# A fused attention and mixture-of-experts kernel: a new order of issue in the first head pair and at the seam between its two halves

## The chip, the cores and the metric

The kernel runs on one core of a Trainium2 chip. A core has TensorE (PE: matmuls; its weight loads, PEld, are listed apart), VectorE (DVE), ScalarE (ACT) and GpSimd (POOL). SyncE (SP) only issues DMAs here. Each engine works through its own instruction stream in order, and engines wait for each other by semaphores. The metric is the time of one run in device microseconds (us); the median of three runs of the kernel before is 529.62 us (529.43 to 530.06).

## The reference, cut to what matters

```
scores = cap * tanh(q @ k.T / sqrt(64) / cap)            # 4 batches, 12 heads, 448 rows, cap 30
attn   = softmax(scores);  x = (attn @ v) as 1792 rows of 768
logits = x @ w_gate;  e_idx = argmax(logits)             # 8 experts, one per row
gate_w = softmax(logits)[e_idx];  eom = sigmoid(x @ w_output_gate)
for e: rows = (e_idx == e)
       out[rows] = gate_w * eom[:, e] * (relu(x[rows] @ w1[e]) @ w2[e])   # 768 -> 1024 -> 768
```

All of it is float32.

## The kernel before, in words

**Attention.** Two heads are worked together as a pair; there are 24 pairs u = 0 to 23, six for each batch. `t_k` and `t_q` turn K and Q of a pair with PE (tiles tk, tq) and split them into a high and a low part (KH, KL, QH, QL). `qk(u, s)` for s = 0 to 3 makes the scores of three double chunks and one single chunk in one of two PSUM buffers `s`, and ACT takes their tanh into `th`, which frees that buffer. The exponentials that turn `th` into `pt` are queued in `pend_exp`, and `flush_exp` issues them, two after every second tanh. `pv(u, c)` multiplies with V into `u`; `u_evac` copies that to `ut` (on ACT for pairs 18 to 21 and 23, on DVE for the others). `presum` adds up the exponentials for the softmax sums, on POOL up to pair 21 and on DVE for pairs 22 and 23, and `sums` reduces them on PE (tile sm).

The transposes of pair u + 2 are issued behind pair u, those of pairs 1 to 3 by hand: in before, those of pair 1 stand behind `qk(0, 2)`.

**Routing.** When a batch is done, `end_of_batch` divides by the sums (rec), makes the gate logits (tg, pg, gm, lg), picks experts, gives every row a place, and writes the row to the DRAM table xs (`row_tr` turns it on PE as trow, `row_out` multiplies on DVE as xr and issues the store) and its place to the tables tab. For batches 0 to 2 these steps are hung into the attention loop by numbers: step x of batch b is run in `slot` at 4·6·(b+1) + 4 + x, four slots to a pair, halves being places in between. For batch 3 the list STEPS gives the order: one word is run behind each chunk of the first expert matmuls.

**Experts.** The rows are grouped in blocks of 128 of one expert. The first five blocks hold rows of batches 0 to 2 only; `early` plans them during pair 21 in six steps (the numbers NXP), so that they can start as soon as attention ends. For a block, `fetch_dma` reads its part of the tables (tc), `gather` works out the row numbers and reads the rows from xs by an indirect DMA on POOL (xg), and `tx` turns and splits them (pt_x, then xh by ACT, xl by DVE). Weights come by `load_raw` on SP (raw, 512 KB a chunk for w1) and are split by ACT and DVE into two planes (wr), several chunks ahead of PE. Blocks 0 and 1 run together (`two1`, tiles php and py).

**The seam** is the passage from pair 22 to `two1`. In before, the SP queue holds there: two row stores, the table reads of blocks 0 and 1, the first weight chunk, V of pair 23, three row stores, five weight chunks. PE holds: the last scores, `pv` of pair 22, `pv` of pair 23, and only then `tx(0)`. Framework pools hand out the buffers; the order on each engine is that of the program text, with no scheduler in between. SP's DMAs use eight semaphores in turn, so a ninth waits for the first.

Of the kernel before, what the change touches and what calls it, by code (L numbers as in the profile page):

```python
# [21 lines left out]
def tile_kernel(ctx: ExitStack, tc, q, k, v, cap, w_gate, w_ogate, w1, w2, out):  # L22
    nc = tc.nc
    B, H, S, D = q.shape
# [5 lines left out]
    NU = B * NP  # L30
    REG = 15 * 128
    NTAB = 128 + E * REG
    NSLOT = 18
    NE = 5
# [16 lines left out]
    AH = 6  # L51
    PZ = 4
    RWP = (9, 10, 12, 13, 14)
    NXP = (7, 7, 7, 7, 7, 7)
    F1 = 5
    F2 = 4
    PRE = 3
    STEPS = 'g s S G x0 X1 l2 c rp3 n4 n5 q e n n n n n n zh'
    WARM = (32, 8, 12, 0)
    RB = 7  # L60
    SP0 = 3
# [2 lines left out]
    UACT = 18  # L64
# [33 lines left out]
    NK = 3  # L98
    SK = NK * 128
# [5 lines left out]
        eng.memset(t[0:64, NK, 1], 0.0)  # L105
        eng.memset(t[64:128, NK, 0], 0.0)

    def load_kv(dst, src, u):
        b, p = divmod(u, NP)
        nc.sync.dma_start(out=dst[:, 0:NK], in_=src[b, 2 * p:2 * p + 2, 0:SK].rearrange("j (p c) d -> p c j d", c=NK))  # L110
        for j in range(2):
            nc.sync.dma_start(out=dst[64 * j:64 * j + 64, NK, j], in_=src[b, 2 * p + j, SK:S])

    def load(u):
        if u >= NU:
            return
        b, p = divmod(u, NP)
        a = ldp.tile([CP, NCH, 2, D], F32, tag="lq", name="lq")
        load_kv(kks[u % 2], k, u)
        nc.sync.dma_start(out=a, in_=q[b, 2 * p:2 * p + 2].rearrange("j (p c) d -> p c j d", c=NCH))  # L120
        ldq[u] = a

# [8 lines left out]
    for t in kks:  # L131
        zero(t, nc.vector)
    load(0)
    nc.sync.dma_start(out=capc, in_=cap.to_broadcast([128, 1]))
    wt = const.tile([128, 1], F32, name="wt")
    nc.scalar.activation(out=wt, in_=wz[:, 0:1], func=ACTF.Exp)

# [140 lines left out]

    pend_exp = []

    def flush_exp():
        while pend_exp:
            dst, th = pend_exp.pop(0)
            nc.scalar.activation(out=dst, in_=th, func=ACTF.Exp, scale=capc)  # L284

    def qk(u, s):
        KH, KL, QH, QL = pl[u]
        if s == 0:
            pt[u] = ptp.tile([128, 2 * NK + 1, S], F32, tag="pt", name="pt")
        n = 2 if s < NK else 1  # L290
        sl = slice(s * 128, (s + 1) * 128)
        ps = ps_s.tile([128, 2, 512], F32, tag="s", name="s")
        if s < NK:
            for i, (x, y) in enumerate(((KH, QH), (KL, QH), (KH, QL))):
                for j in range(2):
                    h = slice(64 * j, 64 * j + 64)
                    nc.tensor.matmul(ps[:, j, 0:S], lhsT=x[h, sl], rhs=y[h], start=(i == 0), stop=(i == 2))  # L297
        else:
            for i, (x, y) in enumerate(((KH, QH), (KL, QH), (KH, QL))):
                nc.tensor.matmul(ps[:, 0, 0:S], lhsT=x[:, sl], rhs=y, start=(i == 0), stop=(i == 2))  # L300
        th = thp.tile([128, 2, S], F32, tag="th", name="th")
        nc.scalar.activation(out=th[:, 0:n], in_=ps[:, 0:n, 0:S], func=ACTF.Tanh, scale=icap)  # L302
        pend_exp.append((pt[u][:, 2 * s:2 * s + n], th[:, 0:n]))
        if s % 2:
            flush_exp()

    def pv(u, c):
        P = pt[u]
# [25 lines left out]

    def u_evac(u):
        t = utp.tile([128, S], F32, tag="ut", name="ut")
        if UACT <= u < NU - 2 or u == NU - 1:
            nc.scalar.activation(out=t, in_=ups.pop(u), func=ACTF.Copy)  # L338
        else:
            nc.vector.tensor_copy(out=t, in_=ups.pop(u))  # L340
        ut[u] = t

    def sums(u):

        b, p = divmod(u, NP)
        if p % 2 == 0:
            return
        r = p // 2
        if r == 0:
            smt[b] = ps_m.tile([128, S], F32, tag="sm", name="sm")  # L350
        for g in range(4):
            nc.tensor.matmul(smt[b][32 * g:32 * g + 32], lhsT=ohc[:, r, :], rhs=s1[u - 1 + g // 2][:, g % 2],
                             start=(r == 0), stop=(r == NP // 2 - 1))
# [10 lines left out]
    def end_of_batch(b):  # L364
# [133 lines left out]
        if b < B - 2:  # L498
            at = {1: [t[2], t[3]], 2: [sums_out], 5: [t[1]], 6: [rws[0]], 9: [gts[0]], 10: [rws[1]], 13: [gts[1]], 14: [rws[2]],
                  15: [logits], 16: [choose], 18: [rws[3]], 21: [rank_mm, place], 22: [rws[4]], 23: [place2], 24: [enter]}  # L500
            at.setdefault(26 if b < B - 3 else 22, []).append(rws[5])
        elif b == B - 2:
            g = early()
            nx = P(next, g, None)
            lds = [P(load_raw, 0, w, c) for w in range(2) for c in range((KD, KF)[w])]
            fd = [P(fetch_dma, i) for i in range(NE)]
            at = {-1: [sums_out], 1: [t[2], t[3]], 2: [t[1], *gts], 3: [logits], 4: [choose],
                  6: [rws[0]], 6.5: [rank_mm, place, place2, enter]}
            for i, x in enumerate(RWP, 1):
                at.setdefault(x, []).append(rws[i])  # L510
            for i, x in enumerate(NXP):
                at.setdefault(x, []).append(nx)
            for x, fs in ((10.5, [fd[0], fd[1], P(set_known, NE), lds[0]]), (15, [P(gather, 0), *lds[1:6], fd[2]]),
                          (16, [P(gather, 1), fd[3], *lds[6:]])):
                at.setdefault(x, []).extend(fs)
        if b < B - 1:
            for x, fs in at.items():
                for f in fs:
# [1 line left out]
            return  # L520
        nx = P(next, late_steps, None)
        do = dict(g=t[2], s=t[0], S=t[1], G=t[3], x=gts[0], X=gts[1], l=logits, c=choose, r=rank_mm, p=place, q=place2,
                  e=enter, n=nx, z=L(P(set_known, NSLOT), P(fetch_dma, NE)), h=lambda: next(rests(), None))
        do.update({str(p): rws[p] for p in range(NP)})
        return [L(*[do[x] for x in w]) for w in STEPS.split()]

# [148 lines left out]
    def rests():  # L675

        full, h, hx, wo = rt["rest"]
        sh = [1, 2, NO, E]
        oh, o2 = M("roh", sh), M("ro2", sh)
        two = lambda x: x.unsqueeze(2).to_broadcast(sh)  # L680
        own = lambda i: metah[:, i, NW:].rearrange("a (z n) -> a z n", z=2)
        tt(wo, wo, over(full, NW), ALU.mult)
        tt(oh, two(hx), irow[:, 0:NO].unsqueeze(1).unsqueeze(3).to_broadcast(sh), ALU.is_equal)
        red(metah[:, 2, 0:NW], wo, ALU.max)
        tt(oh, oh, two(h), ALU.mult)
        tt(o2, oh, full.unsqueeze(1).unsqueeze(1).to_broadcast(sh), ALU.mult)
        red(own(1), oh, ALU.max)
        red(own(2), o2, ALU.max)
        tt(o2, oh, e8.unsqueeze(1).unsqueeze(1).to_broadcast(sh), ALU.mult)
        red(own(0), o2, ALU.max)  # L690
        yield
# [41 lines left out]
            nc.sync.dma_start(out=t4[:, c], in_=tabs[c][bass.ds(off, 128)])  # L733

    def gather(i):
        t4 = tcs.pop(i)
        t = xgp.tile([128, 2], F32, tag="tb", name="tb", bufs=6)
        nc.gpsimd.tensor_tensor(out=t4[:, 0:2], in0=t4[:, 0:2], in1=t4[:, 2:4], op=ALU.add)
        nc.gpsimd.tensor_tensor(out=t, in0=t4[:, 0], in1=t4[:, 1], op=ALU.add)
        ti = xgp.tile([128, 1], U32, tag="ti", name="ti", bufs=6)  # L740
        nc.gpsimd.tensor_scalar(out=ti, in0=t[:, 0:1], scalar1=float(NT), scalar2=None, op0=ALU.add)
        tb[i] = (t, ti)
        n = (B - 1) * S if i < NE else NT + 8
        g = xgp.tile([128, DM], F32, tag="xg", name="xg")
        if i in (1, 3, 4):

            nc.gpsimd.memset(g, 0.0)
        nc.gpsimd.indirect_dma_start(
            out=g, out_offset=None, in_=xs[0:n], in_offset=bass.IndirectOffsetOnAxis(ap=ti, axis=0),
            bounds_check=n - 1, oob_is_err=i not in (1, 3, 4))  # L750
        xg[i] = g
# [13 lines left out]
    def tx(i):  # L765
        if i < NSLOT:
            xg[i] = tr_split(xg[i], KD, "x", 2, xgp)
# [61 lines left out]
    def step():  # L829
        if bg:  # L830
            bg.pop(0)()
# [24 lines left out]
    def slot(u, s):  # L856
        for f in slots.pop(4 * u + s, ()):
            f()

    for u in range(NU):  # L860
        if u > 2:
            load(u + 3)
        qk(u, 0)
        qk(u, 1)
        if u > 0:
            presum(u - 1, 1)
        slot(u, 0)
        if u > 0:
            pv(u - 1, 0)
            pv(u - 1, 1)  # L870
            pv(u - 1, 2)
        if u > 1 and u - 2 != EARLY:
            sums(u - 2)
        slot(u, 1)
        if u in (1, 2):

            prep(u + 1)
            load(u + 3)
        qk(u, 2)
        if u == 0:  # L880
            prep(1)
            load(3)
        slot(u, 2)
        qk(u, 3)
        if u > 0:
            pv(u - 1, 3)
            u_evac(u - 1)
        slot(u, 2.5)
        if u > 1:
            prep(u + 2)  # L890
        if u - 1 == EARLY:
            sums(u - 1)
        load_v(u + 2)
        presum(u, 0)
        slot(u, 3)
# [248 lines left out]
    bg.extend(end_of_batch(B - 1))  # L1144
    pv(u, NK)
    u_evac(u)
    tx(0)
    step()
    sums(u)
    step()  # L1150
    gather(2)

# [92 lines left out]
```

## Time and profile before

| | us |
|---|---|
| median of 3 runs | 529.62 |
| the profiled execution, its own time | 527.99 |
| its span, first to last instruction | 526.3 |
| PE busy | 508.1 (97%) |
| ACT busy | 381.6 (73%) |
| DVE busy | 345.5 (66%) |
| POOL busy | 298.7 (57%) |

The span runs from the first to the last instruction; about 1.7 us of the execution's own time lie around it. Busy time is an average over stages with different limits, so it says little about what an edit in one stage is worth: that is read from the rows of the stage. A clock of 1.00 in the profile is TensorE's full speed, 0.51 about half of it. In a timeline row, the text in brackets is the idle time of the engine just before it and what ended that. "x2" merges instructions that follow each other.

### The profile page before, as it was taken

The numbers are of one execution on the slowest core, as the hardware profiler recorded it, in microseconds if no ns is written. First come the engines' busy times: TensorE is split into PE (matmuls) and PEld (weight loads), VectorE is DVE, ScalarE is ACT, GpSimd is POOL, SyncE is SP. The second block draws the span as 40 slices with busy tenths as digits, with TensorE's granted clock in tenths as the row PEclk, the third lists the DMA queues.
The fourth block names the chain that finished last, engine by engine and source line by source line (L and its number), as shares of the span: only waits on it lengthen the run. The fifth ranks groups of instructions, "written<-read, shape, count | busy, mean of one in ns | idle before, by whom it ended". The sixth has DMA issues, their size and how long they took to land. (4 is left out here: it accounts for less than half of the span.)

```text
span 526.3 us, 10342 instructions
## 1 busy us (share of the span) xinstructions
PE 508.1 (97%) x3197; PEld 361.5 (69%) x3197; DVE 345.5 (66%) x576; ACT 381.6 (73%) x498; POOL 298.7 (57%) x341
## 2 busy tenths in 40 slices
PE   7999999999999989699999999999999999999995
PEld 6555465555655544377999898887878968666692
DVE  3363354965496877599998996975758686545460
ACT  5989897888787978535678886886766787555561
POOL 8988967778987696435254975314737015182001
PEclk9999999999999999899999999999999999999999
DMA  6644434445445316887159636329659959994001
GB/s 148 142 108 102 105 74 106 103 108 111 102 113 132 73 36 189 289 303 219 49 184 389 243 95 206 128 69 386 242 169 391 375 173 368 359 349 167 1 31 49
DMA packets 106189, 91.94 MB, mean 175 GB/s; under 512 B 80770, under 2 KB 88970, under 8 KB 106128
## 3 DMA queue, kind: packets, MB, share of 16 engines
q1 hardware_dynamic: 97392, 58.48, 38.2%
q0 software_dynamic: 8736, 32.74, 17.2%
q8 instruction: 27, 0.44, 0.3%
q14 instruction: 34, 0.28, 0.2%
HBM read 123.68 MB, written 12.04 MB: 258 GB/s over the span
## 5 line engine op out<-in xcount | busy, mean ns | idle before, releaser
L947 DVE TENSOR_TENSOR wr<-raw,wr 128x768 fp32r<-128x768 f32 (+1 forms) x167 | 172.0, 1067 | 68.3 <-ACT wr L946 59.4
L946 ACT ACTIVATE wr<-raw 128x768 fp32r<-128x768 f32 (+1 forms) x167 | 150.2, 936 | 33.0 <-DMA raw<-in_moe_w_dram 12.1
L302 ACT ACTIVATE th<-s,icap 128x896 f32<-128x896 f32 x96 | 84.3, 915 | 27.4 <-PE s L297 19.0
L284 ACT ACTIVATE pt<-th,capc 128x896 f32<-128x896 f32 x96 | 85.7, 947 | 0.0
L968 PE MATMUL py<-wr,hh 128*128 128x384 f32 x352 | 77.3, 340 | 0.0
L968 PE MATMUL php<-wr,xh 128*128 128x512 f32 x264 | 74.8, 404 | 0.0
L1037 POOL DMA_INDIRECT out_dram<-yo,ti x13 | 18.5, 1426 | 86.6 <-ACT yo L1035 62.2
L968 PEld LDWEIGHTS py<-wr,hh 128*128 128x128 f32 x352 | 61.2, 188 | 4.0 <-issue 3.7
L317 PE MATMUL u<-pt,vv 128*64 128x448 f32 x288 | 59.4, 548 | 0.5 <-ACT ut L338 0.5
L968 PEld LDWEIGHTS php<-wr,xh 128*128 128x128 f32 x264 | 47.6, 189 | 12.9 <-issue 2.1
L329 POOL TENSOR_TENSOR pb<-pa,pt 128x896 f32<-128x896 f32 x22 | 46.5, 2113 | 17.0 <-issue 13.7
L333 POOL TENSOR_TENSOR pb<-pb,pt 64x448 f32<-64x448 f32 x44 | 52.1, 1185 | 4.5 <-DMA tab<-ent,posi 1.2
L328 POOL TENSOR_TENSOR pa<-pt 128x896 f32<-128x896 f32 x22 | 46.3, 2104 | 2.3 <-ACT ex L439 0.8
L968 PE MATMUL py<-wr,hl 128*128 128x384 f32 x176 | 44.8, 335 | 0.0
L968 PE MATMUL php<-wr,xl 128*128 128x512 f32 x132 | 41.4, 395 | 0.0
L317 PEld LDWEIGHTS u<-pt,vv 128*64 128x64 f32 x288 | 18.5, 136 | 30.5 <-issue 23.1
L1084 POOL DMA_DIRECT2D rh<-in_moe_w_dram x42 | 23.5, 561 | 22.7 <-issue 16.3
L297 PE MATMUL s<-QH,KH 64*128 64x448 f32 x144 | 31.7, 432 | 1.7 <-ACT th L302 1.7
L968 PEld LDWEIGHTS py<-wr,hl 128*128 128x128 f32 x176 | 31.8, 188 | 0.0
L340 DVE COPY ut<-u 128x448 f32<-128x448 f32 x19 | 11.8, 623 | 29.9 <-PE u L320 29.1
L968 PEld LDWEIGHTS php<-wr,xl 128*128 128x128 f32 x132 | 24.7, 187 | 6.0
L1138 POOL DMA_INDIRECT out_dram<-yh,toh x6 | 6.0, 1008 | 38.0 <-ACT wr L946 10.0
(243 smaller groups left out, 862.6 us busy)
## 6 DMA issues: line engine op xcount, KB each, us to landing
raw<-in_moe_w_dram SPq DMA_DIRECT2D x78, 512.0 KB
raw<-in_moe_w_dram SPq DMA_DIRECT2D x104, 384.0 KB
rh<-in_moe_w_dram POOLq DMA_DIRECT2D x18, 512.0 KB
rh<-in_moe_w_dram POOLq DMA_DIRECT2D x24, 384.0 KB
lq<-in_q_dram SPq DMA_DIRECT2D x24, 224.0 KB
kk<-in_k_dram SPq DMA_DIRECT2D x24, 192.0 KB
vv<-in_v_dram SPq DMA_DIRECT2D x24, 192.0 KB
xs<-xr SPq DMA_DIRECT2D x18, 224.0 KB
```

The source lines that it names most:

```text
L284: nc.scalar.activation(out=dst, in_=th, func=ACTF.Exp, scale=capc)
L297: nc.tensor.matmul(ps[:, j, 0:S], lhsT=x[h, sl], rhs=y[h], start=(i == 0), stop=(i == 2))
L302: nc.scalar.activation(out=th[:, 0:n], in_=ps[:, 0:n, 0:S], func=ACTF.Tanh, scale=icap)
L317: nc.tensor.matmul(ups[u][64 * j:64 * j + 64], lhsT=V[:, c, j, :], rhs=P[:, 2 * c + j], start=(c == 0), stop=False)
L328: eng.tensor_tensor(out=a, in0=P[:, 0:2], in1=P[:, 2:4], op=ALU.add)
L329: eng.tensor_tensor(out=s1[u], in0=a, in1=P[:, 4:6], op=ALU.add)
L333: eng.tensor_tensor(out=s1[u][h, j], in0=s1[u][h, j], in1=P[h, 2 * NK], op=ALU.add)
L946: nc.scalar.activation(out=t[:, 0, 0:F], in_=raw, func=ACTF.Copy)
L947: nc.vector.tensor_tensor(out=t[:, 1, 0:F], in0=raw, in1=t[:, 0, 0:F].bitcast(F32), op=ALU.subtract)
L968: nc.tensor.matmul(ps[g][:, 0:n], lhsT=st[:, c], rhs=w[:, z, g * n:(g + 1) * n], start=(c == 0 and st is hi and z == 0), stop=(c == (KD, K ...
L1037: nc.gpsimd.indirect_dma_start(out=out, out_offset=bass.IndirectOffsetOnAxis(ap=ti, axis=0), in_=y, in_offset=None, bounds_check=NT - 1, o ...
L1084: nc.gpsimd.dma_start(out=d, in_=src[bass.ds(e, 1)].rearrange("e (k p) f -> p (e k) f", p=128)[:, c], **kw)
```

## The change

In the first pair, the two small DMAs of the first K load and the load of `cap` are issued by ACT and no longer by SP; PE makes the transposes of pair 1 ahead of `qk(0, 2)`; and after the second tanh ACT makes one exponential, not two.

At the seam, two of the planner's six steps come two and three slots later, behind row stores; the table reads of block 1, its gather and weight chunks 1 to 5 come behind the last three row stores; block 0's row numbers are worked out earlier on POOL (`index`), apart from its gather (`take`); `tx(0)` stands ahead of `pv` of pair 23; the `ut` copy of pair 21 goes from ACT to DVE; `sums(23)` becomes a step of STEPS, behind the first chunk of `two1`; and STEPS puts the last two row stores and the late planner's steps elsewhere.

```
-    NXP = (7, 7, 7, 7, 7, 7)
+    NXP = (7, 7, 7, 7, 9, 10)
-    STEPS = 'g s S G x0 X1 l2 c rp3 n4 n5 q e n n n n n n zh'
+    STEPS = 'g U s S G x0 X1 l2 c 3r p4 n5 n q e nn n n nn zh'
-    def load_kv(dst, src, u):
+    def load_kv(dst, src, u, eng=None):
...
         for j in range(2):
-            nc.sync.dma_start(out=dst[64 * j:64 * j + 64, NK, j], in_=src[b, 2 * p + j, SK:S])
+            (eng or nc.sync).dma_start(out=dst[64 * j:64 * j + 64, NK, j], in_=src[b, 2 * p + j, SK:S])
...
-        load_kv(kks[u % 2], k, u)
+        load_kv(kks[u % 2], k, u, nc.scalar if u == 0 else None)
...
-    nc.sync.dma_start(out=capc, in_=cap.to_broadcast([128, 1]))
+    nc.scalar.dma_start(out=capc, in_=cap.to_broadcast([128, 1]))
...
-    def flush_exp():
-        while pend_exp:
+    def flush_exp(keep=0):
+        while len(pend_exp) > keep:
...
         if s % 2:
-            flush_exp()
+            flush_exp(int((u, s) == (0, 1)))
...
-        if UACT <= u < NU - 2 or u == NU - 1:
+        if UACT <= u < NU - 3 or u == NU - 1:
...
-            for x, fs in ((10.5, [fd[0], fd[1], P(set_known, NE), lds[0]]), (15, [P(gather, 0), *lds[1:6], fd[2]]),
-                          (16, [P(gather, 1), fd[3], *lds[6:]])):
+            for x, fs in ((10.5, [fd[0], P(set_known, NE)]), (11, [lds[0], P(index, 0)]), (14, [fd[1]]),
+                          (15, [P(take, 0), fd[2], *lds[1:4]]), (16, [P(gather, 1), *lds[4:6], fd[3], *lds[6:]]),
+                          (18.5, [P(tx, 0)])):
...
     def gather(i):
+        index(i)
+        take(i)
+
+    def index(i):
...
+    def take(i):
+        ti = tb[i][1]
...
-        qk(u, 2)
         if u == 0:
             prep(1)
             load(3)
+        qk(u, 2)
...
     u_evac(u)
-    tx(0)
-    step()
-    sums(u)
     step()
     gather(2)
```

Three places, as the engines' streams show them. First ACT at the start of the program, a piece of the difference (KH and QH are the first pair's split, th the tanhs, pt the exponentials):

```order
+L112 DMA kk_126<-in_k_dram 64x64 x2
+L134 DMA capc<-in_cap_dram 128x1
 L136 ACT_TABLE_LOAD
 L136 ACTIVATE wt<-wz 128x1
...
 L302 ACTIVATE th<-s,icap 128x896 x2
-L284 ACTIVATE pt<-th,capc 128x896 x2
-L302 ACTIVATE th<-s,icap 128x896
-L302 ACTIVATE th<-s,icap 128x448
-L284 ACTIVATE pt<-th,capc 128x896
+L284 ACTIVATE pt<-th,capc 128x896
+L302 ACTIVATE th<-s,icap 128x896
+L302 ACTIVATE th<-s,icap 128x448
+L284 ACTIVATE pt<-th,capc 128x896 x2
```

ACT now issues three DMAs before anything else, and the second exponential stands behind the third and fourth tanh.

Then PE at the seam, a piece of the difference (the first L320 row ends `pv` of pair 22, the two rows on vv_130 are `pv` of pair 23, tg and sm belong to the last batch's gates and sums):

```order
 L320 MATMUL u<-pt,vv_129 128x448
+L768 MATMUL pt_x<-ident,xg 128x128 x6
 L317 MATMUL u<-pt,vv_130 64x448 x6
 L320 MATMUL u<-pt,vv_130 128x448
-L760 MATMUL pt_x<-ident,xg 128x128 x6
 L389 MATMUL tg<-ut,wg 32x448 x4
+L976 MATMUL php<-wr,xh 128x512 x4
+L976 MATMUL php<-wr,xl 128x512 x2
 L352 MATMUL sm<-pb,ohc 32x448 x4
```

The six transposes of block 0 moved ahead of the whole `pv` of pair 23, and the first expert chunk ahead of the last sums.

Last SP at the seam, before, from the last of the eight table reads that stand there (tc) to weight chunk 1 (raw_1):

```order
L733 DMA tc<-tab_111 128x2
L703 TENSOR_LOAD meta
L703 ISA x2
L710 ISA
L710 DMA raw_0_112<-in_moe_w_dram 128x1024
L110 DMA vv_130<-in_v_dram 128x6x64
L112 DMA vv_130<-in_v_dram 64x64 x2
L490 DMA xs<-xr 448x1x128 x3
L710 ISA
L710 DMA raw_1_113<-in_moe_w_dram 128x1024
```

and now, from the last of four table reads on:

```order
L734 DMA tc<-tab_111 128x2
L110 DMA vv_130<-in_v_dram 128x6x64
L112 DMA vv_130<-in_v_dram 64x64 x2
L704 TENSOR_LOAD meta
L704 ISA x2
L711 ISA
L711 DMA raw_0_112<-in_moe_w_dram 128x1024
L490 DMA xs<-xr 448x1x128 x3
L731 TENSOR_LOAD meta
L731 ISA x2
L734 ISA
L734 DMA tc<-tab_108 128x2
```

Four table reads instead of eight stand ahead of the three row stores. Behind them come eight table reads, and only then weight chunk 1, which stood right behind the stores.

## Rows read from the trace of the kernel before

**Rows 1.** Busy time by stretch: us, PE, PEld, DVE, ACT, POOL, PEclk, DMA share, GB/s.

```profile
26.00:178.00 152.00, 151.13 (x974) 85.40 (x970) 92.10 (x171) 128.26 (x158) 124.71 (x81) 1.00 0.46 102
178.00:212.00 34.00, 30.88 (x184) 16.01 (x182) 25.96 (x76) 27.50 (x39) 24.10 (x21) 1.00 0.47 125
211.70:216.20 4.50, 0.14 (x2) 0.12 (x2) 3.35 (x4) 2.21 (x3) 2.95 (x3) 1.00 1.02 356
217.00:220.40 3.40, 3.40 (x17) 0.86 (x18) 1.02 (x2) 1.36 (x4) 1.50 (x4) 0.51 0.38 102
220.40:270.00 49.60, 48.59 (x262) 40.76 (x262) 44.61 (x118) 27.86 (x39) 16.88 (x24) 1.00 0.55 177
270.00:520.00 250.00, 250.00 (x1593) 202.18 (x1591) 170.78 (x188) 174.23 (x233) 104.65 (x138) 1.00 0.63 229
```

**Rows 2.** Who waited for whom, PE, whole run: us in total, times, longest.

```profile
PE pt_x L760 <- DMA xg<-xs,ti: 4.4, 1, 4.4
PE s L297 <- ACT th L302: 1.7, 2, 1.2
PE tk L271 <- DVE xr L487: 1.6, 2, 1.2
```

**Rows 3.** Timeline of PE, first pairs: start us, us, instruction, idle before it.

```profile
6.27 0.61 PE L258 MATMUL tq<-ident,lq 112*128 112x112 f32 x4 [0.29 <-DMA lq<-in_q_dram]
...
13.40 0.47 PE L297 MATMUL s<-QH,KH 64*128 64x448 f32 x2 [1.21 <-ACT th L302]
...
20.65 0.48 PE L297 MATMUL s<-QH,KH 64*128 64x448 f32 x2
```

**Rows 4.** Timeline of ACT, first pairs.

```profile
8.69 1.91 ACT L302 ACTIVATE th<-s,icap 128x896 f32<-128x896 f32 x2 [1.23 <-PE s L297]
10.49 1.97 ACT L284 ACTIVATE pt<-th,capc 128x896 f32<-128x896 f32 x2
...
19.20 1.53 ACT L302 ACTIVATE th<-s,icap 128x896 f32<-128x896 f32 x2 [0.17 <-PE s L297]
```

**Rows 5.** Timeline of PE at the seam.

```profile
208.33 2.48 PE L317 MATMUL u<-pt,vv 128*64 128x448 f32 x12
210.74 1.02 PE L320 MATMUL u<-pt,vv 128*128 128x448 f32 x2
216.12 0.85 PE L760 MATMUL pt_x<-ident,xg 128*128 128x128 f32 x6 [4.36 <-DMA xg<-xs,ti]
216.89 1.72 PE L389 MATMUL tg<-ut,wg 128*32 128x448 f32 x8
```

**Rows 6.** Timeline of SP's DMA issues at the seam.

```profile
194.50 5.16 SPq L733 DMA_DIRECT2D tc<-tab  x8
200.47 0.34 SPq L710 DMA_DIRECT2D raw<-in_moe_w_dram  x1
...
203.06 1.98 SPq L490 DMA_DIRECT2D xs<-xr  x3
205.26 3.31 SPq L710 DMA_DIRECT2D raw<-in_moe_w_dram  x5
```

**Rows 7.** Timeline of POOL at the seam.

```profile
192.94 2.35 POOL L333 TENSOR_TENSOR pb<-pb,pt 64x448 f32<-64x448 f32 x2
...
199.74 4.33 POOL L333 TENSOR_TENSOR pb<-pb,pt 64x448 f32<-64x448 f32 x2
...
209.00 1.14 POOL L748 DMA_INDIRECT xg<-xs,ti  x1 [3.43 <-DMA raw<-in_moe_w_dram]
```

**Rows 8.** Timeline of DVE at the seam.

```profile
204.26 0.69 DVE L836 CAST wr<-raw 128x1024 fp32r<-128x1024 f32 x1 [1.19 <-DMA raw<-in_moe_w_dram]
...
208.98 1.15 DVE L328 TENSOR_TENSOR pa<-pt 128x896 f32<-128x896 f32 x1
...
212.75 2.36 DVE L947 TENSOR_TENSOR wr<-raw,wr 128x1024 fp32r<-128x1024 f32 x2
...
221.77 2.36 DVE L947 TENSOR_TENSOR wr<-raw,wr 128x1024 fp32r<-128x1024 f32 x2 [3.33 <-ACT wr L946]
```

More of the change, by code (lines that the diff above doesn't have):

```diff
@@ L522, in end_of_batch @@
         do = dict(g=t[2], s=t[0], S=t[1], G=t[3], x=gts[0], X=gts[1], l=logits, c=choose, r=rank_mm, p=place, q=place2,
-                  e=enter, n=nx, z=L(P(set_known, NSLOT), P(fetch_dma, NE)), h=lambda: next(rests(), None))
+                  e=enter, n=nx, U=P(sums, NU - 1), z=L(P(set_known, NSLOT), P(fetch_dma, NE)), h=lambda: next(rests(), None))
         do.update({str(p): rws[p] for p in range(NP)})
```

## The prediction

> **What bounds the kernel now.** I read the stage table first [rows 1]: PE is busy 151.13 of 152 us in attention, 250 of 250 us in the experts, 48.59 of 49.60 behind the seam. ACT and DVE have room nearly everywhere; in 220 to 270 DVE is at 44.61 of 49.60, which I keep for later. So PE's own waits are the time that can be won, and the list of waits over the whole run names them [rows 2]: 4.4 us once for the gathered rows of block 0 (xg), 1.7 for tanhs, 1.6 for row products (xr). Then I read the timelines at the two places that the change touches. At the seam `pv` of pair 23 ends at 211.76 (210.74 + 1.02), and PE stands until 216.12 [rows 5]. From 217.0 to 220.4 the granted clock is 0.51, that is 1.2 in place of 2.4 GHz, and 1.00 ahead of that [rows 1]: at half speed 3.40 us do 1.73 us of work, so the wait costs another 1.67 us. In the first pair PE waits 1.21 us for a tanh at 13.40 [rows 3]; ACT runs without a pause from 8.69 to 19.20, but for 0.17 us [rows 4].
>
> The change aims at all of these. What each part is worth follows, in the times of the profiled execution.
>
> **First pair.** The three DMAs that leave SP bring the first Q load forward; PE's `tq` waits 0.29 us for that load [rows 3], so the first tanh comes 0.3 earlier. On ACT the three issues stand ahead of work that is idle until 5.5 us, so I price them at nothing; without that cover they would cost about three issues of 0.34 us [rows 6]. Next, one exponential (half of 1.97 with overlap, 0.93) moves behind the third tanh [rows 4], which is what PE waits for at 13.40: the wait of 1.21 shrinks by 0.93, and with the 0.3 PE is 1.23 us ahead. That holds only while ACT keeps up, and ACT's total work is the same: its chain is ahead only by 0.3 and by the pause of 0.17, 0.47 in all. The next place where PE needs it is 20.65 [rows 3]: the tanh at 19.20 would start at 18.73 and end 0.96 later (half of 1.91), at 19.7, so PE starts there 0.95 earlier. The transposes of pair 1, moved ahead, fill PE's waits and add nothing. Behind 20.65 PE has no wait for ACT left, so the lead stays. Ends: 0.47 (ACT sets all) to 1.23; I take 0.95, worked out for the very row.
>
> **Seam, when the gather starts.** The gather of block 0 is issued at 209.00 after 3.43 us of waiting [rows 7]. The profile puts this down to a weight load, but by the program it waits for the row stores of batch 2, since it reads xs. The last three are issued until 205.04 (203.06 + 1.98) [rows 6], so the stores land 3.96 us after the last issue. In the new order half of the eight table reads (2.58 of 5.16 us) is no longer ahead of them: 202.46. SP also begins earlier, since the two planner steps now stand behind the row products for which it (and PE, 1.2 us) waits [rows 2]; I take 1.2 for that: 201.3, and landed at 205.2, or 206.4 without it. POOL must be free too: its two additions take from 199.74 to 204.07, and the row numbers another 1.5 until 205.57 (209.00 - 3.43). The row numbers now come first, and wait for four table reads that are issued earlier; the additions took 2.35 at the pair before and 4.33 here [rows 7], so POOL is free between 203.6 and 205.6. The gather starts at about 204.8 (bounds 203.6 and 206.4).
>
> **When it lands.** Before, 7.12 us passed from its issue to PE's start, while five weight chunks (2.6 MB), issued from 205.26 on, kept the DMA full at 356 GB/s [rows 1, 6]. Now these are issued behind eight table reads, some 5 us after the stores. Bounds: 7.12, and 2.24 (1.14 of issue, and 0.39 MB at 356 GB/s). The nearest row is the weight chunk issued into a light queue: issued at 200.47, used by DVE at 204.26, 3.8 us [rows 6, 8]; a gather issues 0.8 longer (1.14 against 0.34) and moves a quarter less (0.3 us): 4.3. So `tx(0)` starts at 209.0 or so, 7.1 us earlier than 216.12.
>
> That is not all gain: `pv` of pair 23 (208.33 to 211.76, 3.43 us) used to run ahead of the wait and now runs behind it [rows 5]. Net 3.7 us. The bounds: PE itself can reach `tx(0)` at 206.6 at the earliest (208.33 less 1.2 for xr and 0.5 for a copy that moves from ACT to DVE), 6.1 us net; with 206.4 and 7.12 it is 213.5 and a loss of 0.8. In both cases what PE wins ahead of `tx(0)` only makes its wait there longer, so I don't add it. Behind the waiting PE stand `pv(23)`, the gate products and the first chunk; the sums' products change places with that chunk, at no cost while planes are ready.
>
> **The clock.** PE's wait is then 209.0 - 206.6 = 2.4 us. A wait of 1.2 us (for xr) left the clock at 1.00 in 178 to 212, one of 4.36 brought it to 0.51 [rows 1, 2]. 2.4 lies between, a little nearer to the short one: I take 1.0 of the 1.67 us as won back; ends 0 and 1.67.
>
> **VectorE behind the seam.** DVE's `xl` now waits for `tx(0)` and stands ahead of the sums of pair 23 (208.98 to 212.75, 3.8 us), and these ahead of the splits that feed PE [rows 8]. Before, DVE then stood 3.33 us until 221.77; this hole can take most of it. Upper end: all 3.8 are paid, since DVE is at 90% until 270 [rows 1]. Lower end: a gain of 1.0, all of PE's idle time in that stretch (49.60 - 48.59), as the planner's later steps and the table entry now come behind `two1`. I take a loss of 1.0. The longer STEPS way of the planner costs nothing as long as blocks 5 and up are not due, 40 us later; the weight chunks issued 1 to 2 us later are covered by several chunks of lead, and would otherwise cost PE that much.
>
> **Sum.** -0.95 - 3.7 - 1.0 + 1.0 = -4.65 us. The profiled execution took 527.99 (a span of 526.3 and 1.7 around it), so about 523.3 there. It lies 1.6 under the median of the runs shown; carried over to that, 529.62 - 4.65 gives 525.0.
>
> **Rivals.**
>
> *The gather lands late all the same.* If the weight chunks weren't what held it up, their absence saves little. For: between its issue and `tx(0)` the 0.39 MB needed only 1.1 us at 356 GB/s of the 7.12. Against: the lone chunk's 3.8 us. If the gather only shared the DMA half and half, it loses 1.1 us to the chunks and takes 6.0 now: `tx(0)` at 210.8, 5.3 earlier, net 1.9, a wait of 4.2 us and so no clock won: -0.95 - 1.9 + 1.0 = -1.85, 527.8. (The Trainium skill, "DMA: Bandwidth & Descriptors", section on queues, rings and completion order, says just that: each DMA engine goes round its queue rows packet by packet, so that POOL's ring would not stand behind SP's backlog. By that rule the time is 527.8; no row here separates the two.)
>
> *VectorE takes it back.* All 3.8 are paid and the clock still falls: -0.95 - 3.7 + 3.8 = -0.85, 528.8, which is no change that can be measured. For: 44.61 of 49.60. Against: the hole of 3.33.
>
> *Slower: PE waits with `pv(23)` behind it.* If `tx(0)` comes less than 3.43 us earlier, PE loses by the new order what it had as filler. With the start's 0.95 and DVE's 1.0 the point is a `tx(0)` later than 212.6; at 214.8 (the stores landing no earlier, with part of the weight backlog again in front) it is -0.95 + 2.1 + 1.0 = +2.15, 531.8. For: POOL was busy or waiting without a break from 199.74 on, and its additions may stretch again. Against: SP is rid of 2.58 us for certain.
>
> **Chances.** The forecast 0.60 (its own range 522 to 527), the late gather 0.18 (527 to 528.6), VectorE 0.12 (528 to 530), slower 0.10 (530.5 to 533). The range 521.8 to 529.6 leaves out the slower case and some 5% below. A difference of 0.2% (1.06 us) is about what a measurement of this kernel can tell. Faster by more: 0.58 + 0.16 + 0.04 = 0.78; slower by more: the slower case and 0.01 of VectorE's, 0.11; the same: 0.11.
>
> **What would show it.** In the new profile PE starts the row at 20.65 about 1 us earlier, and the list of waits has no 1.2 for xr at the seam. The three row stores are issued by 201.3 less the start's lead, the gather near 204, `tx(0)` near 208 with a wait of 1.5 to 3.5 in front. A clock of 1.00 through the seam, or a shorter stretch at half speed, shows that term; new PE waits for DVE between 210 and 240 would show VectorE's. The forecast is wrong if the gather still takes over 6 us to land, or if PE's waits return as many small ones in `two1`.

## The result: 0.9% slower, and the profile after

The changed kernel takes 534.64 us (median of 6 runs) against 530.02 for the kernel before in the same session: a ratio of 1.0088, 95% interval 1.007 to 1.0105. The prediction had 525.0 and ended its range at 529.6, so it was wrong in sign. The profiled execution has a span of 532.8 us (526.3 before).

First PE's list of waits, as in [rows 2] (us in total, times, longest). The 4.4 for the gathered rows (xg) has fallen to 1.2. In its place stand waits that were small or absent: 4.3 at once for xr, 2.4 for ble, 1.7 for ut, 1.6 for xl.

```profile
PE tq L258 <- DVE xr L487: 4.5, 2, 4.3
PE ph L976 <- DVE ble L536: 2.4, 1, 2.4
PE tg L389 <- ACT ut L338: 1.7, 1, 1.7
PE pt_x L768 <- DVE xl L770: 1.6, 1, 1.6
PE pt_x L768 <- DMA xg<-xs,ti: 1.2, 1, 1.2
```

Next the stage table, as in [rows 1] (us, PE, PEld, DVE, ACT, POOL, PEclk, DMA share, GB/s). PE's idle time in 178 to 212 grew from 3.1 to 5.3 us, in 220.4 to 270 from 1.0 to 4.1; attention before it and the experts behind it stayed full. The half clock (1.2 in place of 2.4 GHz) left the seam and came back behind the two longest of the new waits: 0.50 in 194.3 to 198.8, 0.58 in 249.8 to 253.7.

```profile
26.00:178.00 152.00, 151.16 (x975) 85.57 (x974) 91.36 (x171) 128.75 (x159) 125.63 (x82) 1.00 0.47 103
178.00:212.00 34.00, 28.72 (x165) 15.78 (x163) 27.49 (x73) 24.85 (x35) 21.14 (x21) 0.90 0.35 83
194.34:198.84 4.50, 4.50 (x20) 3.16 (x20) 3.70 (x6) 2.40 (x3) 4.34 (x3) 0.50 0.25 52
220.40:270.00 49.60, 45.53 (x237) 36.05 (x236) 38.20 (x95) 25.42 (x37) 14.20 (x20) 0.97 0.55 182
249.80:253.70 3.90, 3.90 (x11) 3.06 (x12) 1.50 (x7) 0.00 (x0) 0.67 (x1) 0.58 0.54 183
270.00:520.00 250.00, 250.00 (x1591) 205.23 (x1590) 177.92 (x212) 177.06 (x234) 105.07 (x140) 1.00 0.62 228
```

Then the timeline of PE at the places of [rows 3] and [rows 5] (start us, us, instruction, idle before it). The lead at 20 us is 0.65, and it is still 0.65 at 183 us. `tx(0)` comes at 213.13, 2.99 earlier than before; but `pv` of pair 23 and a wait for ut follow, and the first expert chunk (php) starts at 219.90, only 0.13 ahead of 220.03. From there to block 2's first product (ph) it takes 29.9 us, against 25.7 before; these are the rows of before:

```profile
220.03 1.32 PE L968 MATMUL php<-wr,xh 128*128 128x512 f32 x4
...
245.75 0.39 PE L968 MATMUL ph<-wr,xh 128*128 128x512 f32 x1
```

and these the rows now:

```profile
20.00 0.47 PE L297 MATMUL s<-QH,KH 64*128 64x448 f32 x2 [0.28 <-ACT th L302]
...
194.34 1.01 PE L258 MATMUL tq<-ident,lq 112*128 112x112 f32 x4 [4.29 <-DVE xr L487]
...
213.13 0.88 PE L768 MATMUL pt_x<-ident,xg 128*128 128x128 f32 x6 [1.25 <-DMA xg<-xs,ti]
...
219.01 0.96 PE L389 MATMUL tg<-ut,wg 128*32 128x448 f32 x8 [1.66 <-ACT ut L338]
219.90 1.20 PE L976 MATMUL php<-wr,xh 128*128 128x512 f32 x4
...
249.80 0.48 PE L976 MATMUL ph<-wr,xh 128*128 128x512 f32 x1 [2.43 <-DVE ble L536]
```

What held xr up stands in DVE's timeline. These are planner steps five and six, in the places that the change gave them:

```profile
187.99 2.13 DVE L536 TENSOR_TENSOR boh<-boh,bo 1x40 f32<-1x40 f32 x1
190.15 2.12 DVE L543 SCALAR_TENSOR_TENSOR bo<-irow,bval 1x40 f32<-1x40 f32 x1
192.30 1.17 DVE L536 TENSOR_TENSOR bo<-bo,boh 1x40 f32<-1x40 f32 x1
193.50 0.18 DVE L533 TENSOR_REDUCE meta<-bo 1x5 int32<-1x40 f32 x1
193.62 0.67 DVE L487 TENSOR_TENSOR xr<-trow,rec 112x512 f32<-112x512 f32 x1
...
194.77 2.05 DVE L536 TENSOR_TENSOR meta<-bch,bsm 1x4 int32<-1x4 f32 x1
```

Forty numbers take 2.13 us; the same operation took 0.19 at 185.95. POOL's timeline beside it:

```profile
187.97 2.10 POOL L328 TENSOR_TENSOR pa<-pt 128x896 f32<-128x896 f32 x1
190.15 2.07 POOL L329 TENSOR_TENSOR pb<-pa,pt 128x896 f32<-128x896 f32 x1
192.30 2.33 POOL L333 TENSOR_TENSOR pb<-pb,pt 64x448 f32<-64x448 f32 x2
194.70 2.10 POOL L328 TENSOR_TENSOR pa<-pt 128x896 f32<-128x896 f32 x1
```

Each long DVE instruction ends within 0.05 us of a POOL addition (190.12 and 190.07, 192.27 and 192.22, 196.82 and 196.80; 193.47 is where the first of the two halves ends). The reduction and xr, which reads PSUM, are not slowed. The kernel before shows one such case in the planner, not among its rows above; here is DVE's row, and below it POOL's, which starts 0.08 us earlier:

```profile
188.67 2.04 DVE L535 TENSOR_TENSOR meta<-bch,bsm 1x4 int32<-1x4 f32 x1
```

```profile
188.59 2.10 POOL L328 TENSOR_TENSOR pa<-pt 128x896 f32<-128x896 f32 x1
```

The Trainium skill states this, "SBUF — State Buffer", section "Who interferes with whom": a DVE instruction with two SBUF inputs contends with a GpSimd instruction that reads SBUF, and the one that comes second blocks until the other is done. The trace agrees, with 2.04 to 2.13 us against 0.19.

### The profile page after: what moved, and what is told of

Its sections match the earlier page's. It is cut to its first block, busy times and chain, and to the rows that moved or that the text cites. A ratio compares the mean times of both kernels' runs of the same rounds, so it can differ in the third digit from the quotient of the medians.

```text
span 532.8 us, 10342 instructions
## 1 busy us (share of the span) xinstructions
PE 510.3 (96%) x3197; PEld 363.2 (68%) x3197; DVE 349.6 (66%) x577; ACT 382.6 (72%) x497; POOL 294.5 (55%) x341
## 5 line engine op out<-in xcount | busy, mean ns | idle before, releaser
L1045 POOL DMA_INDIRECT out_dram<-yo,ti x13 | 19.8, 1527 | 88.8 <-ACT yo L1043 63.8
L333 POOL TENSOR_TENSOR pb<-pb,pt 64x448 f32<-64x448 f32 x44 | 50.1, 1139 | 4.1 <-DMA tab<-ent,posi 0.8
L474 POOL DMA_INDIRECT tab<-ent,posi x16 | 15.6, 975 | 24.1 <-DVE ent L472 14.5
```

The lines of the kernel that those rows point to most:

```text
L333: eng.tensor_tensor(out=s1[u][h, j], in0=s1[u][h, j], in1=P[h, 2 * NK], op=ALU.add)
L1045: nc.gpsimd.indirect_dma_start(out=out, out_offset=bass.IndirectOffsetOnAxis(ap=ti, axis=0), in_=y, in_offset=None, bounds_check=NT - 1, o ...
```

## The experiments

Each time is a median of 5 to 12 runs; "before" was run beside it on the same chip. The ratio can differ from the quotient of the two medians by up to 0.2% (1 us).

| run | us | before | ratio (95%) |
|---|---|---|---|
| the change | 534.64 | 530.02 | 1.0088 (1.007 to 1.0105) |
| e1 planner back | 534.08 | 529.73 | 1.008 (1.0054 to 1.0106) |
| e2 planner alone | 530.68 | 529.73 | 1.0019 (1.0005 to 1.0034) |
| e3 planner and STEPS back | 528.21 | 529.73 | 0.9977 (0.9963 to 0.9991) |
| e4 start alone | 529.14 | 529.73 | 0.9993 (0.9981 to 1.0004) |
| e5 sixth step late | 525.75 | 529.33 | 0.9939 (0.9926 to 0.9951) |
| e6 tx(0) behind pv | 527.89 | 529.33 | 0.9964 (0.9947 to 0.9981) |
| e8 no shift | 528.05 | 529.33 | 0.9986 (0.9972 to 1.0001) |
| e9 STEPS back alone | 533.35 | 529.62 | 1.0052 (1.0033 to 1.0071) |
| e10 copy first, tx(0) behind pv | 525.51 | 529.62 | 0.991 (0.9892 to 0.9928) |
| e11 copy first | 526.22 | 529.62 | 0.9927 (0.9908 to 0.9946) |
| e12 weights first | 529.76 | 529.62 | 1.0 (0.9987 to 1.0014) |
| e13 new STEPS, planner out of the way | 530.37 | 529.71 | 1.0029 (1.0007 to 1.0052) |
| e14 STEPS alone | 533.47 | 529.71 | 1.0087 (1.0067 to 1.0107) |

**e1**, in the changed kernel:

```
-    NXP = (7, 7, 7, 7, 9, 10)
+    NXP = (7, 7, 7, 7, 7, 7)
```

> The changed kernel with the planner's last two steps back at slot 7. Theory (VectorE held up by GpSimd): in the changed kernel four of the moved steps' instructions took 2.13, 2.12, 1.17 and 2.05 us in place of 0.15 to 0.20, each ending with a GpSimd addition. Back at slot 7 all but one (about 2 us) are done before GpSimd starts to add: PE's wait for xr falls from 4.3 to about 1.2 us, the stretch at half clock at 194 to 199 us is gone, and the time is 4.0 to 5.0 us under the changed kernel, near 530. Rival (the queues at the seam, weight chunks behind the table reads): the wait for xr is only slack, and the time stays within 1.5 us of the changed kernel's 534.6.

The mechanism came as expected, the time did not. One DVE instruction of 2.03 us is left and PE waits 1.2 for xr; but PE then stands 5.4 us before `tx(0)`, with the clock at 0.79 over 206 to 222. PE came to that wait 4.7 us earlier than in the change (207.16 in place of 211.88), and `tx(0)` only 0.6 earlier. The gather here took 6.41 us from its issue to `tx(0)`.

**e2**, the same edit the other way, in the kernel before:

```
-    NXP = (7, 7, 7, 7, 7, 7)
+    NXP = (7, 7, 7, 7, 9, 10)
```

> The kernel before with only the planner's last two steps moved to slots 9 and 10. Theory (VectorE held up by GpSimd): the same long instructions of about 2 us as in the changed kernel, a PE wait for xr of 4 us or more, and since the row stores and so the gather hang on these rows, the gather comes about 4 us later too: 533 to 535. Rival (the new order at the seam is to blame as a whole): the move alone costs under 1 us, 529.5 to 531.

The wait for xr is 3.3 us, as in the theory, yet it costs 0.95 us: in the old order most of it comes out of the 4.4 at xg, which falls to 2.1, and behind that shorter wait the clock stays at 1.00. So the rival's number, by the theory's mechanism.

**e3**, e1 and besides:

```
-    STEPS = 'g U s S G x0 X1 l2 c 3r p4 n5 n q e nn n n nn zh'
+    STEPS = 'g s S G x0 X1 l2 c rp3 n4 n5 q e n n n n n n zh'
...
     step()
+    sums(u)
+    step()
     gather(2)
```

> The changed kernel with the planner at slot 7, and with STEPS and the place of the last sums as in the kernel before. Theory (late rows): in the changed kernel the last batch's rows 3 to 5 come one to two chunks later, and the expert products of block 2 wait 2.4 us for the buffer that row 5 holds, the turns of block 2 1.6 us; these waits and the half clock behind them (1.5 us) go: 4 to 5 us under the run with the planner alone back, near 526. Rival (weight chunks land late): the waits inside the first expert pair stay as waits for wr or raw, and the gain is under 1.5 us, 529 or more.

The waits for ble and xl are gone, and the time is 5.9 us under e1; of these, 2.67 are `tx(0)`, at 209.87 in place of e1's 212.54, which STEPS can't have moved. The theory held for the waits, and the total was 528.2, not 526. PE still stands 2.9 us for xg and has the half clock behind it.

**e4**, the three edits of the first pair in the kernel before.

> The kernel before with the three edits of the first pair alone. Theory: PE is 0.65 us ahead in the changed kernel at the scores of 20 us and keeps that until 183 us, so 0.4 to 0.9 us under the kernel before. Rival (the lead is lost at the wait for the gathered rows, which depends on SP and GpSimd): no change within 0.2 us.

0.6 us under the kernel before, not certain (the interval reaches 1.0004); the trace has PE at 20.09 in place of 20.65. The wait for lq grew from 0.29 to 0.7: moving the three small DMAs won nothing there. By the rows it is the exponential that won; no run has it alone.

**e5**, e3 with `NXP = (7, 7, 7, 7, 7, 14.5)`.

> The run with STEPS back, but with the planner's sixth step at slot 14.5 (behind row 5 of batch 2), where GpSimd has done its additions; the fifth stays at slot 7. Theory (VectorE held up by GpSimd): the one instruction of 2.04 us that was left there at 188 us takes 0.2, and PE's wait for xr of 1.25 us goes, with the row stores 1 to 2 us earlier. Since PE then only stands longer before the gathered rows unless these come earlier too, the time falls by 0.3 to 1.5 us under the run with STEPS back (528.2). Rival (SP's queue sets the stores): the stores come no earlier, and the time is the same within 0.3 us.

3.6 us under the kernel before. The wait for xr is at most 0.2, but one of 1.43 for KL, which I had not expected, stands in its place: PE is no earlier than in e3 (`pv` of pair 21 starts at 194.75, there at 194.05). Behind it the seam is close to what I had forecast (timeline of PE):

```profile
194.16 0.65 PE L483 MATMUL trow<-ident,ut 128*112 128x128 f32 x4 [1.43 <-DVE KL L252]
...
209.68 0.88 PE L768 MATMUL pt_x<-ident,xg 128*128 128x128 f32 x6 [2.06 <-DMA xg<-xs,ti]
210.49 2.48 PE L317 MATMUL u<-pt,vv 128*64 128x448 f32 x12
...
216.64 1.20 PE L976 MATMUL php<-wr,xh 128*128 128x512 f32 x4
...
242.56 0.39 PE L976 MATMUL ph<-wr,xh 128*128 128x512 f32 x1
```

`tx(0)` at 209.68 (forecast 209.0) behind a wait of 2.06 (forecast 2.4), no half clock, and 25.9 us from php to ph. Against e3 `tx(0)` is only 0.19 us earlier; most of what is won is the clock, with `pv` of pair 23 in 2.48 us and not in 4.17. That the wait is 0.88 shorter than in e3, and the clock stays, is in part luck: for 0.69 of it PE only came later, behind the wait for KL.

**e6**, e5 with `tx(0)` called behind `u_evac` of pair 23, as in the kernel before, and no longer at 18.5.

> The run with the sixth step late, and with tx(0) back behind pv of pair 23. Theory (PE has to have filler while the gather lands): PE stood 2.9 us before tx(0) in the run with STEPS back, then did pv of pair 23 at half clock for 4.17 instead of 2.48 us; with pv first it fills the wait, PE waits under 1 us, the clock stays at 1.00, and the first expert chunk comes 2 to 4 us earlier: 524 to 526. Rival (the early turn was the gain of the change): the chain from the gathered rows through xh and xl to the first chunk is now what is late, and the time is the same or up to 1 us longer than with tx(0) ahead.

Neither: 2.1 us over e5, and 527.9 in all. PE no longer waits for xg at all, but now 3.6 us for ut before tg. On ACT the copy of ut stands behind two weight splits (211.92 to 214.4); the profile lets the first wait for DVE's sums and the second for its chunk.

**e7**, the changed kernel with POOL's additions of pairs 20 and 21 made memsets.

```
+            if u in (20, 21):
+                for _ in range(4):
+                    eng.memset(s1[u], 5.0)
+                return
```

> The changed kernel, with GpSimd's additions for pairs 20 and 21 replaced by memsets that read nothing (so the softmax sums of these two pairs are left out, which changes the rows and experts of the last batch a little). Theory (GpSimd's additions and VectorE's instructions with two operands in SBUF exclude each other): the four planner instructions that took 1.2 to 2.1 us take 0.14 to 0.2 again, and PE's wait of 4.3 us for xr goes, though GpSimd is still busy there. Rival (the wait is for a semaphore or for GpSimd being busy with anything): they stay as long as the GpSimd instruction beside them.

Read from the trace alone (the rows of the last batch go to other experts, so the time says nothing). POOL was busy over the whole stretch, and the planner ran at full speed:

```profile
187.75 7.05 POOL L330 MEMSET pb<- 128x896 f32 x8
```

```profile
189.82 0.19 DVE L540 TENSOR_TENSOR boh<-boh,bo 1x40 f32<-1x40 f32 x1
190.05 0.19 DVE L547 SCALAR_TENSOR_TENSOR bo<-irow,bval 1x40 f32<-1x40 f32 x1
```

A POOL that only writes does not hold DVE up; one that adds two tiles does. PE's wait for xr fell from 4.3 to 1.2, so 3.1 us of it came from these collisions. That settles the first cause.

**e8**, e1 with `U` put into the first word (`'gU s S ...'`) and one more `step()` ahead of the experts, so that the words are not shifted while their new order stays.

> The changed kernel with the planner at slot 7, the new order of STEPS kept, but the last sums in the first word and two words run ahead of the expert products, so that rows 3 to 5 come two chunks earlier than in the changed kernel. Theory (late rows): the lateness is what costs, not the order of the words; the waits of 1.7 and 2.4 us go, and the time is within 1 us of the run with STEPS back (528.2). Rival (the order of planner steps against rows costs): the wait of block 2's products stays at 1 us or more, 531 to 534.

528.05, as e3: the waits are gone. What costs is that the words come later, not how they are ordered.

**e9**, the changed kernel with STEPS and sums back alone (the second diff of e3).

> The changed kernel with STEPS and the place of the last sums as in the kernel before, and the planner's last two steps left at slots 9 and 10. Theory (two losses, the late rows the larger): the waits of 1.6 and 2.4 us in the first expert pair and the half clock behind them go, 4 to 5.5 us under the changed kernel: 529 to 530.5, and 1 to 2 us over the run with both back (528.2), since the wait of 4.3 us for xr stays. Rival (the losses only show together): the time stays within 2 us of the changed kernel, 532.5 or more.

The rival's time. The waits inside the first expert pair are indeed gone (0.7 and 0.3 are left), but in this execution planner step five began 0.07 us behind POOL's first addition, and five of its instructions met one each (the first three here):

```profile
189.95 2.03 DVE L543 SCALAR_TENSOR_TENSOR bval<-blo,ereg 1x8 f32<-1x8 f32 x1
191.90 0.15 DVE L536 TENSOR_TENSOR bhi<-blo,bnb 1x8 f32<-1x8 f32 x1
192.09 2.08 DVE L536 TENSOR_TENSOR bo<-bhi,irow 1x40 f32<-1x40 f32 x1
194.20 1.17 DVE L536 TENSOR_TENSOR boh<-boh,bo 1x40 f32<-1x40 f32 x1
```

PE's wait for xr was 8.2 us. So this wait has no fixed size: 3.3 in e2, 4.3 in the change, 8.2 here.

**e10**, e6 with `split_to(SP0)` called behind `tx(0)`, no longer ahead of `pv`; **e11**, e5 with it behind `u_evac`.

```
-    split_to(SP0)
     bg.extend(end_of_batch(B - 1))
     pv(u, NK)
     u_evac(u)
     tx(0)
+    split_to(SP0)
```

> The run with tx(0) behind pv of pair 23, and with the splits of weight chunks 1 and 2 (split_to) called behind u_evac and tx(0), no longer ahead of pv: on ACT the copy of ut of pair 23 and xh stand ahead of two splits that wait for their chunks. Theory (ACT's order made PE wait 3.6 us for ut there): tg comes at about 211.3 in place of 214.9 us, the clock stays at 1.00, and the first expert chunk comes at 213 to 215 us in place of 218.0: 523 to 525. Rival (weight chunks land too late in any order): the gain returns as waits for wr or raw in the first expert pair, 526 to 528.

> The run with the sixth step late (tx(0) ahead of pv of pair 23), with the same two splits called behind u_evac. Theory: PE's wait of 1.1 us for ut before tg goes, 0.5 to 1.1 us under 525.75. Rival (weight chunks): the same within 0.4 us.

e10 is the best ratio found, 0.991. In its profile (span 521.3, of its fastest run) PE has no listed wait above 0.35 us between 194 and 233 us, though 1.44 for KL just ahead of that, and the first chunk starts at 213.86. Its median is no lower than e5's within the spread. e11's wait for ut fell from 1.1 to 0.6, and the time stayed.

**e12**, e5 with SP's order of the kernel before:

```
-                          (15, [P(take, 0), fd[2], *lds[1:4]]), (16, [P(gather, 1), *lds[4:6], fd[3], *lds[6:]]),
+                          (15, [P(take, 0), *lds[1:6], fd[1], fd[2]]), (16, [P(gather, 1), fd[3], *lds[6:]]),
```

(and `fd[1]` taken out of 14).

> The run with the sixth step late, and with weight chunks 1 to 5 right behind the three row stores on SP, ahead of the table reads, as in the kernel before. Theory (a backlog of weight chunks holds the gather and its stores up): the stores or the gather land later, from the gather's issue to PE's tx(0) it takes 5.5 us or more in place of 4.3, PE's wait for xg grows by 1.5 to 4 us, with half clock behind it: 527.5 to 530. Rival (each DMA queue gets its turn whatever stands on the other): tx(0) is as early as without, and the time is 525 to 526.5.

4 us over e5 (3.7 when each is set against the kernel before beside it). The gather is issued at 205.63 (205.35 in e5) and takes 6.79 us to `tx(0)` in place of 4.33; timelines of POOL and of PE:

```profile
205.63 1.38 POOL L756 DMA_INDIRECT xg<-xs,ti  x1 [3.12 <-DMA xs<-xr]
```

```profile
212.42 1.54 PE L768 MATMUL pt_x<-ident,xg 128*128 128x128 f32 x6 [5.06 <-DMA xg<-xs,ti]
213.89 3.78 PE L317 MATMUL u<-pt,vv 128*64 128x448 f32 x12
```

So a backlog of weight chunks does hold the gather up. To have it behind the gather is what this order gains: without that, nothing is left of it (ratio 1.0).

**e13**, the changed kernel with `NXP = (7, 7, 7, 7, 7, 14.5)` alone; **e14**, the new STEPS alone in the kernel before.

> The changed kernel with one edit: the planner's fifth step back at slot 7 and the sixth at 14.5; STEPS as in the changed kernel. Theory (the late rows of the last batch cost by themselves): PE waits about 1.6 us for block 2's turns and 2.4 us for its products, against 1.0 us in all for the old words, so 3 us over the run with the sixth step late and STEPS back (525.75): 528 to 530. Rival (the words cost only with a late gather): 525.5 to 526.5.

> The kernel before with the new STEPS alone, the last sums as the word U behind the first expert chunk. Theory: the same waits of 1.6 and 2.4 us as in the changed kernel, in place of 0.7 and 0.3: 2 to 4 us over the kernel before, 531.5 to 533.5. Rival (no cost by itself): 529 to 530.5.

The theory both times, e13 0.4 us above its range: 4.2 us over e5 (each against the kernel before beside it), and 3.8 over the kernel before. The PE rows of e14 show the two waits, DVE what ends the second:

```profile
242.17 0.44 PE L760 MATMUL pt_x<-ident,xg 128*128 128x128 f32 x2 [1.64 <-DVE xl L762]
...
250.13 0.47 PE L968 MATMUL ph<-wr,xh 128*128 128x512 f32 x1 [2.43 <-DVE ble L535]
```

```profile
249.29 0.69 DVE L487 TENSOR_TENSOR xr<-trow,rec 112x512 f32<-112x512 f32 x1
249.90 0.20 DVE L535 TENSOR_TENSOR ble<-lek,bnb 1x64 f32<-1x64 f32 x1
```

The list names ble, but what ends 0.15 us before ph is xr (249.98). In the code the turned rows of the last batch (trow) and ph use one PSUM buffer (`hph`, one deep). Row 5 is the ninth chunk's word in the old list (its eleventh word, two of which run ahead of the experts) and the eleventh chunk's in the new one (its twelfth, with one ahead). There, xr stands on DVE behind two weight splits and the planner's step, and block 2 is next on PE. The first wait is of the same kind: xl, which ends it, stands on DVE behind a weight split (239.70) and the xr of row 3 (240.84).

## Why the prediction was wrong, step by step

The runs, each median against that of the kernel before beside it: the change is at +4.62; with the planner back at slot 7 (e1) +4.35; with the old words (e9) +3.73; with both back (e3) -1.52. So the two edits, which I had priced at a gain and at nothing, cost 6.1 us together, and taking only one of them back wins little. Each has a cost of its own: 0.95 for the planner (e2) and 3.76 for the words (e14) in the kernel before, where PE's wait for the gather took up most of the first, and 5.2 for the planner with the old words in the new order (e9 over e3). With the sixth step out of the way at 14.5, where it stood neither before nor in the change, the rest of the change is at -3.58 (e5); the new words make that +0.66 (e13), and the planner at 9 and 10 makes it +4.62.

- **"The two planner steps now stand behind the row products ... I take 1.2 for that."** This step failed, with the wrong sign. I saw that row products would no longer stand behind planner steps, and not what the steps would meet in their new place: POOL's additions of pair 20, from 187.97 on. PE's wait for xr became 4.29 us, and behind it the clock was at 0.50 for 4.5 us. The last three row stores were issued until 204.76, not until 201.3, and the gather at 208.69, not at 204.8. Nor was PE's 1.2 there to be had: in e7, where nothing collides, PE still waits 1.2 for xr, and in e5 1.43 for KL. The row of 2.04 us at 188.67 was in the trace of before, and the prediction passes over it; it was the one planner instruction that met an addition there. POOL's 4.33 in place of 2.35 [rows 7] fits the same cause in the other direction: DVE's additions of pair 22 run beside it from 200.02 on, and in the change, where no such DVE instruction does, the same pair takes 2.35. I only noted that it "may stretch again".
- **"The longer STEPS way of the planner costs nothing", "the sums' products change places with that chunk, at no cost".** This step failed too. I weighed what is in the words, and not that a word of its own for the sums and one word fewer ahead of the experts move every later word by two chunks. The bound that I named (blocks 5 and up, 40 us later) was the wrong reader; block 2 needs the buffer at the end of `two1`, where PE waited 2.43 us for it and, ahead of that, 1.64 for xl; php to ph took 29.9 us in place of 25.7.
- **The start.** 0.65 in the trace, 0.6 in e4, for 0.95. The mechanism fits for the exponential; the 0.3 from lq was not there (its wait grew from 0.29 to 0.63).
- **When the gather lands.** Right where its issue ends ahead of the chunks: 4.44 us from issue (208.69) to `tx(0)` in the change, 4.33 in e5, for 4.3 forecast from one weight chunk. That it might not end ahead of them (e1) I had not seen. The rival of the late gather falls with e12: with chunks ahead 6.79, without 4.33. The Trainium skill's rule named with that rival (engines go round their queue rows) is not borne out as an equal share here: half and half would cost 1.1, e12 shows 2.46.
- **The slower rival** had its point right: `tx(0)` came at 213.13, later than its 212.6. But in the change PE itself came late and waited only 1.25 there; to wait with `pv(23)` behind it is the case of e1. Its price was put on late stores and not on DVE.
- **The clock.** For the seam it went as forecast, by a price set between two waits that I had seen: the wait of 2.06 us left it at 1.00 (e5), one of 2.94 had half clock behind it (e3: `pv` took 4.17 in place of 2.48). In the change it was lost at two places where I had no wait; the one of 2.43 had half clock behind it there and in e13 (0.56), and none in e14 (1.00).
- **VectorE behind the seam.** In e5 the stretch from php to ph took 25.9 us, 25.7 before: the 1.0 that I charged was not paid, but 1.1 (1.7 in the change) for ut behind weight splits on ACT, which I had not seen.

Why e1, whose streams are the same as e3's as far as `tx(0)`, had its gather take 6.41 us in place of 4.19, can be read from the traces side by side, though no run tries it by itself. In e1 the issue of the gather took 2.13 us (1.16 in e3) and ended at 208.26, 0.41 us after SP had begun the weight chunks (207.85). Counted from the end of its issue, the gather took 2.97 to 3.30 us until `tx(0)` in the eight runs where that end lies ahead of the chunks or at most 0.10 us behind their start (the change, e3, e5, e7, e8, e9, e11, e13), 4.28 in e1, and 5.38 to 6.41 in the five where it lies behind all of them (before, e2, e4, e12, e14). So the new order has little to spare: the gather's issue ended 0.38 us ahead of the chunks in e5, and 0.04 in e11. Still open is why the issue itself took 2.13 us in e1 and 2.00 in e8. That the same thing made e1 take 533 to 536 us in eight of nine runs and 529.5 in one is likely, but only one of them has a trace.

## What to carry to other kernels

Before moving small VectorE instructions, look at what GpSimd runs at the new place: two operands in SBUF beside a GpSimd addition cost up to that addition's whole length, and tiny instructions that wait in turn cost one addition each. A row far longer than its twins in the trace before can be such a place already. In a list that is run one word a chunk, an added word moves all that follow; look for the buffer that the last of them holds, and who needs it next. Filler ahead of a wait pays only if nothing behind it comes late by it: `tx(0)` behind `pv` lost 2.1 us (e6) until ACT's order was changed too, and then came out level with e5 (e10). And when one transfer has to be issued ahead of another on a second queue, look at how much time lies between them.

## What the runs showed of the hardware

- DVE's instructions with two SBUF operands and POOL's additions exclude each other for a whole instruction: 0.19 us became 2.13 beside an addition of 2.10, and not where POOL only wrote (e7).
- A gather on POOL's queue issued behind 2.6 MB of weight chunks on SP's took 6.79 us to its use (e12), and 4.33 ahead of them (e5).
